# One plan of step places over the attention and gate stage of a packed-attention, SwiGLU and bilinear kernel

## The chip, the cores and the metric

The kernel runs on one core of one Trainium2 chip. The metric is device time in microseconds (us) of one execution, as the median over several runs. All work, the conversion of the weights included, is inside that time.

## The reference

The inputs are q, k and v of 8 batches, 8 heads, 576 positions and 64 values a head, and 32 packing queries p per head; then weights for two dense layers.

```python
p_packed = softmax(p @ k.T / 8) @ v            # 32 rows a head
x  = softmax(q @ p_packed.T / 8) @ p_packed    # 576 rows a head
x  = x laid out as 4608 tokens x 512
xn = x / sqrt(mean(x * x) + 1e-6) * rms_g
y  = (silu(xn @ w_gate) * (xn @ w_val)) @ w_out      # 512 -> 1536 -> 512
out = ((y @ w1) * (y @ w2)) @ w3 @ w_out2            # 512 -> 1024 -> 512
```

The weights arrive as 64-bit words and are turned to float32 on the chip. A dense product is done as three float32r products of high and low parts (hi x hi, hi x lo, lo x hi).

## The kernel before, in words

Only the first third of the kernel, the front and the dense gate stage of the 8 batches, is touched. What comes behind it (the product with `w_out`, the products of the weights, the last two layers) stays as it is.

**The work of a batch** has three parts, and each is a Python generator whose `yield`s cut it into steps:

- `pack(b)`, 7 steps. Steps 0 and 1: scores of p against k on TensorE (L216, all 32 matmuls in step 0), their maximum on VectorE and exponential on ScalarE, for one half of the heads each. Step 2: the load of k of batch b+2, transposes (L232) and their evictions (L236, L239). Step 3: the product with v (L247) and the load of v of batch b+1. Step 4: eviction (L256). Step 5: a transpose (L259), the block-diagonal `bdP1T` (L264) and `gP1T` (L266). Step 6: the Gram matrix `G` (L276, L279).
- `unpack(b)`, 18 steps. Step 0: scores of q (L305) and two 32 x 32 transposes on VectorE (L309). Step 1: the load of q of batch b+2, a maximum on VectorE; steps 2 to 4: subtraction, exponential and the other half. Steps 5 and 6: sums and reciprocals on VectorE (L321 to L323), a product on GpSimd (L324). Steps 7 and 8: transposes on VectorE (L329), one of them also shifted over partitions by two DMAs into `turned` (L332, L333). Step 9: the product with `G` on TensorE (L345); steps 9 and 10: its elementwise products `sq` on VectorE (L350). Step 11: from batch 3 on the two halves of `sq` are added on GpSimd (L354). Step 12: the sums of squares as matmuls against a column of ones (L361): 5 on the added halves, or 10 on both halves where nothing was added; `ssq` on VectorE (L363). Step 13: the power -0.5 on GpSimd (L366). Steps 14 and 15: transposes of it on TensorE (L371), the scaling on VectorE (L373). Steps 16 and 17: the split into `ah` and `al` (L59, L60).
- `dense_units`, 48 steps a batch, 6 blocks of 8. A step is 6 matmuls of 128x288 into one of 4 PSUM banks (L435). An even step ends with a tanh on ScalarE (L441) and a product on VectorE (L442), an odd one with `ht`: on VectorE in batch 0 (L447), on ScalarE and GpSimd in the others (L450, L451). Every fourth step an `ht` tile (3 buffers) is full, and its store goes out 8 steps later. After the fourth step of a block, `wb_unit` makes the weight products of the next block (L393 on TensorE, `wbh` on ScalarE, `wbl` on VectorE; both by the helper `split`, L59 and L60).

**Beside these** run two streams of weight conversion. A c step brings a load and two ScalarE operations (L115, L116), a d step the two VectorE operations (L122, L123) and the GpSimd addition (L125) for the gate and value weights; a d step that finds no converted words makes the c step itself. An o step is a whole conversion of a tile of `w_out`, w1 or w2: a load of 512 KB three tiles ahead, the same five operations, and a later store.

**The order** of all instructions is the order in which the Python code makes them, for each engine and for the DMA queue of SyncE (SP), which issues every load and store in order. Ahead of the dense stage a string names the generators one after the other ("p", "u": pack and unpack of batch 0; "P", "U": of batch 1; "c", "d": conversion; "l": loads of k, v, q of batches 1 to 3 in that order; "w": the first `wb_unit`; "x": four matmuls of the identity into a bank that nobody reads). Then `planned` runs the dense steps and after step n takes every step that has n in its list, in the order of the lists:

```python
    def planned(main, *others):
        for n, _ in enumerate(main):
            for at, gen in others:
                for _ in range(at.count(n)):
                    next(gen, None)
        for _, gen in others:
            drain(gen)
```

In the kernel before there is one such plan for batches 0 and 1 (steps 0 to 95), one call of `planned` for each of batches 2 to 6 (steps 0 to 47), and one for batch 7 with the first loads of the stage behind. While batch b is in the dense stage, `unpack(b+1)` and `pack(b+2)` are taken.

Of the kernel before, what the change touches and what calls it, by code (L numbers as in the profile page):

```python
# [16 lines left out]
B, H, S, D = 8, 8, 576, 64  # L17
NP = 32
R = 5
# [13 lines left out]
def packed_attention_swiglu_bilinear(ctx: ExitStack, tc, qT, kT, v, v_end, pT, rms_g, w_gv, w_out,  # L33
# [21 lines left out]
    def bank():  # L55
        return ps.tile([128, 512], F32, tag="gv", name="gv", bufs=4)
# [39 lines left out]
    def load_v(b):  # L96
        if b < B:
# [1 line left out]
            nc.sync.dma_start(out=vt[:, :R - 1], in_=v[b])  # L99
            nc.sync.dma_start(out=vt[64:, R - 1], in_=v_end[b])  # L100
            raw["v", b] = vt

    def load64(src):
# [23 lines left out]
    def converting(jobs, take):  # L130


        n64 = ahead64[0]
        ahead = [load64(src) for src, *_ in jobs[:n64]]
        yield
        for i, job in enumerate(jobs):
            take(ahead.pop(0), *job[1:])
            if i + n64 < len(jobs):
                ahead.append(load64(jobs[i + n64][0]))
            yield  # L140
# [145 lines left out]
    def unpack(b):  # L286
# [13 lines left out]
        for a, t in enumerate(ts):  # L300
            for c in range(NC):
                for e in range(2):
# [4 lines left out]
                                     start=True, stop=True, tile_position=(64 * e, r))  # L307
# [31 lines left out]
        for a in range(2):  # L339
            for e in range(2):  # L340
                for c in range(NC):
                    r = place(c, e)
                    k = r if b == 0 else 32 * c
                    x = turned[k:k + 32] if b and e else a2T[k:k + 32, e]
                    nc.tensor.matmul(ts[e][r:r + 32, a, :HALF], lhsT=G[k:k + 32, b % 2, e],  # L345
                                     rhs=x[:, HALF * a:HALF * a + HALF],
                                     start=True, stop=True, tile_position=(k, r))
        over.add(("G", b))
        for e in range(2):
            nc.vector.tensor_tensor(out=halves(sq[:, e]), in0=ts[e][:, :, :HALF], in1=halves(a2T[:, e]),  # L350
                                    op=ALU.mult)
            yield
        if b > 2:
            nc.gpsimd.tensor_tensor(out=sq[:, 0], in0=sq[:, 0], in1=sq[:, 1], op=ALU.add)  # L354
        yield
        ssq = att.tile([128, R], F32, tag="ssq", name="ssq")
        rinv = att.tile([128, R], F32, tag="rinv", name="rinv")
        t = slot("at")
        for r in range(R):
            for e in range(1 if b > 2 else 2):  # L360
                nc.tensor.matmul(t[:, 0, 2 * r:2 * r + 2], lhsT=sq[:, e, T0[r]:T0[r] + 128], rhs=ones,  # L361
                                 start=(e == 0), stop=(e == 1 or b > 2), skip_group_check=True)
        nc.vector.tensor_scalar(out=ssq, in0=t[:, 0, :2 * R].rearrange("p (r j) -> p r j", j=2)[:, :, 0],  # L363
                                scalar1=0.0, scalar2=1e-6, op0=ALU.max, op1=ALU.add)
        yield
# [19 lines left out]
    def wb_unit(b, g):  # L385
        gP1T = res["gP1T", b]
        while not all((g, c) in converted for c in range(NC)):
            next(gvd)
        t = slot("at")
        for c in range(NC):  # L390
            for e in range(2):
                r = place(c, e)
                nc.tensor.matmul(t[r:r + 32, e, :], lhsT=gP1T[64 * e:64 * e + 64, c, :],  # L393
                                 rhs=wgv[64 * e:64 * e + 64, c, :, 256 * g:256 * g + 256],
                                 start=True, stop=True, tile_position=(64 * e, r), skip_group_check=True)
        hi = dp.tile([128, 2, 512], F32R, tag="wbh", name="wbh", bufs=2)
        lo = dp.tile([128, 2, 512], F32R, tag="wbl", name="wbl", bufs=2)
        split(hi, lo, t, nc.vector)
        wb[b, g] = (hi, lo)
# [4 lines left out]
    def store_later(steps, **dma):  # L404
        held.append([steps, dma])

    def stores():
        for x in held:
            x[0] -= 1
        while held and held[0][0] <= 0:  # L410
            nc.sync.dma_start(**held.pop(0)[1])
# [2 lines left out]
        while held:  # L414
            stores()

    FIRST = [(b, g) for b in range(2) for g in range(6)]
    blocks = FIRST + [(b, g) for b in range(2, B) for g in range(6)]
    follow = dict(zip(blocks, blocks[1:]))

    def dense_units(blocks):
        for b, g in blocks:
            ah, al = res["a2n", b]
            hi, lo = wb.pop((b, g))
            for f in range(2):
                ht = dp.tile([128, 2, HALF], F32, tag="ht", name="ht", bufs=3)
                for hf in range(2):
                    th = dp.tile([128, HALF], F32, tag="th", name="th", bufs=3)
                    vl = dp.tile([128, HALF], F32, tag="vl", name="vl", bufs=2)
                    for i in range(2):  # L430
                        t = bank()
                        n = 0
                        for w, x in ((hi, ah), (hi, al), (lo, ah)):
                            for e in range(2):
                                nc.tensor.matmul(t[:, :HALF],  # L435
                                                 lhsT=w[:, e, 256 * i + 128 * f:256 * i + 128 * f + 128],
                                                 rhs=x[:, e, HALF * hf:HALF * hf + HALF],
                                                 start=(n == 0), stop=(n == 5))
                                n += 1
                        if i == 0:  # L440
                            nc.scalar.activation(out=th, in_=t[:, :HALF], func=AF.Tanh, scale=0.5)  # L441
                            nc.vector.scalar_tensor_tensor(out=th, in0=th, scalar=1.0, in1=t[:, :HALF],  # L442
                                                           op0=ALU.add, op1=ALU.mult)
                            stores()
                            yield 0.75
                    if b == 0:
                        nc.vector.scalar_tensor_tensor(out=ht[:, hf], in0=th, scalar=0.5, in1=t[:, :HALF],  # L447
                                                       op0=ALU.mult, op1=ALU.mult)
                    else:
                        nc.scalar.activation(out=vl, in_=t[:, :HALF], func=AF.Copy, scale=0.5)  # L450
                        nc.gpsimd.tensor_tensor(out=ht[:, hf], in0=th, in1=vl, op=ALU.mult)  # L451
                    if hf == 1:
                        store_later(4, out=hT_d[2 * g + f, :, S * b:S * b + S],
                                    in_=ht.rearrange("p a n -> p (a n)"))
                    yield 0.75
                    if (f, hf) == (0, 1) and (b, g) in follow:
                        wb_unit(*follow[b, g])

    def batch(b):
        return dense_units([(b, g) for g in range(6)])  # L460

    def some(gen, n):
        for _ in range(n):
            yield next(gen, None)

    def drain(gen):
        for _ in gen:
            pass
# [33 lines left out]
    def wb_first():  # L502
        wb_unit(0, 0)
        yield

    def later():
        for b in (1, 2, 3):
            load_k(b)
            yield
            if b < 3:  # L510
                load_v(b)
                yield
            load_q(b)
            yield

    jobs = [(w_out[128 * i:128 * i + 128, :], wo_d[128 * i:128 * i + 128, :]) for i in range(NF)]
    for n in range(16):
        r, c = GROUPS[n // 4]
        w, kk = ((w1, r), (w1, r + 2), (w2, r), (w2, r + 2))[n % 4]
        jobs.append((w[128 * kk:128 * kk + 128, 512 * c:512 * c + 512], w12_d[n]))  # L520
    ow = converting(jobs, out_weight)
    def spin():
        while True:
            t = bank()
            for _ in range(4):
                nc.tensor.matmul(t[:, :128], lhsT=ident, rhs=ident, start=True, stop=True)
            yield

    gens = dict(x=spin(), p=pack(0), u=unpack(0), c=gvw, d=gvd, w=wb_first(), l=later(), P=pack(1), U=unpack(1),
                Q=pack(2), V=unpack(2), R=pack(3), o=ow)  # L530
    for x in ("xppxdxpcpxdcpdpcxcdcuducpduxuxuxcxd"
              "xculdxuxxxxwxucudxxuuuxuPPxuuuuxudPl"):
        next(gens[x], None)
    for x in "pu":
        drain(gens[x])
    PLAN = [("P", [6, 9, 12, 21]),
# [8 lines left out]
    planned(dense_units(FIRST),  # L545
            *((at, gens[x] if x != "o" else some(ow, len(at))) for x, at in PLAN))
    for x in "PUQVRcdl":
        drain(gens[x])

    PACK = [7, 7, 16, 31, 32, 40, 43]  # L550
    UNPACK = [0, 1, 3, 4, 6, 11, 13, 15, 17, 24, 24, 25, 31, 32, 40, 41, 42, 44]
    for b in range(2, B - 1):
        others = [(UNPACK, unpack(b + 1)), ([9, 18, 23, 28, 35, 46], some(ow, 6))]
        if b + 2 < B:
            others.insert(0, (PACK, pack(b + 2)))
        planned(batch(b), *others)
    drain(ow)
    flush()
    att_ctx.close()
# [100 lines left out]
    def halved(w, hi, lo):  # L660
# [1 line left out]
            split(*behind.pop(), nc.vector)  # L662
            staged.append(0)
        behind.append((hi, lo, as_f32(w)))

    ORDER = (0, 5, 4, 6, 1, 3, 2)
# [149 lines left out]
    flush()  # L818
    p2_ctx.close()
    cv2_ctx.close()  # L820

    wt = ctx.enter_context(tc.tile_pool(name="wt", bufs=1, side="right"))
# [293 lines left out]
```

## Time and profile before

| | |
|---|---|
| median of 3 runs | 1357.19 us (1355.32 to 1358.64) |
| the profiled execution | 1356.66 us, its span 1354.4 us, granted clock 0.994 |
| TensorE matmul busy | 1327.6 us, 98% of the span |
| TensorE weight load busy | 1130.0 us, 83% |
| VectorE busy | 837.4 us, 62% |
| ScalarE, GpSimd busy | 580.1 us, 581.2 us |
| share of the chain that ended last | TensorE 89%, VectorE 4%, ScalarE 2%, GpSimd 2%, DMA 2% |

The profile is of one execution. Times are from the start of its span. Busy times of TensorE are modelled for their ends, so idle time and the granted clock (1 is 2.4 GHz, 0.5 is 1.2 GHz) tell more than its busy share. A wait is put down to what was released last. The dense stage of batch 0 starts at 49.72 us, that of batch 7 near 450 us (the first load of its plan, L572, is issued at 450.44).

### The profile page before, as it was taken

The page shows a single profiled execution, that of the slowest core. Times are in us where ns is not written, and L with a number is a line of the kernel's source. Part 1 is how long each engine was busy: PE and PEld are TensorE (multiplying, and loading weights), DVE is VectorE, ACT ScalarE, POOL GpSimd, SP SyncE. Part 2 cuts the span into 40 slices and gives each one's busy share as a digit, 9 for nine tenths or more (in the row PEclk, how much of TensorE's full clock was granted, in tenths as well). Part 3 has the DMA queues.
Part 4 walks back from the last instruction along what each step waited for, and adds up shares of the span by engine and source line. Part 5 has one row for each costly group of instructions (what it writes and reads, how often), then busy time and mean ns, then how long its engine had stood idle before and what let it go on. Part 6 is the DMA issues. An engine that isn't in the chain of part 4 may idle for free.

```text
span 1354.4 us, 23647 instructions
## 1 busy us (share of the span) xinstructions
PE 1327.6 (98%) x9022; PEld 1130.0 (83%) x9022; DVE 837.4 (62%) x1261; ACT 580.1 (43%) x1117; POOL 581.2 (43%) x490
## 2 busy tenths in 40 slices
PE   7979999999999999999999999999999999999998
PEld 6768878788788888888888888888888888899998
DVE  6785676676766557726375564566468357457444
ACT  5544566666766656525243342125015103305113
POOL 3341446556556543203131213447345535535543
PEclk9989999999999999999999999999999999999999
DMA  8664637666352467734299875656755855787875
GB/s 309 252 223 171 238 135 263 230 217 216 116 190 104 149 220 245 236 106 140 86 372 389 337 261 210 228 206 226 279 198 199 283 191 210 242 310 258 280 270 186
DMA packets 88705, 304.03 MB, mean 224 GB/s; under 512 B 9872, under 2 KB 14992, under 8 KB 74384
## 3 DMA queue, kind: packets, MB, share of 16 engines
q1 hardware_dynamic: 88592, 302.52, 63.3%
q8 instruction: 71, 1.16, 0.3%
q14 instruction: 42, 0.34, 0.1%
HBM read 223.87 MB, written 76.55 MB: 222 GB/s over the span
## 4 chain that ended last, share of the span: by engine, by line
PE 89%; DVE 4%; ACT 2%; POOL 2%; DMA 2%; issue 1%; SPq 0%; ACTq 0%; DVEq 0%; POOLq 0%
PE gv L435 20%; PE at L641 14%; PE gv L954 13%; PE at L954 13%; PE gv L641 7%; PE gv L1048 6%; PE at L1048 5%; PE gv L742 3%; PE at L393 3%; POOL sl L60 1%; DMA hT_d<-ht 1%; PE at L361 1%; PE at L345 1%; PE at L247 1%; DVE wbl L60 1%
## 5 line engine op out<-in xcount | busy, mean ns | idle before, releaser
L451 POOL TENSOR_TENSOR ht<-th,vl 128x288 f32<-128x288 f32 x168 | 141.8, 851 | 142.7 <-ACT vl L450 60.3
L435 PE MATMUL gv<-ah,wbh 128*128 128x288 f32 x768 | 175.3, 309 | 3.8 <-DVE ht L447 1.8
L435 PEld LDWEIGHTS gv<-ah,wbh 128*128 128x128 f32 x768 | 121.4, 189 | 55.1 <-issue 22.6
L435 PE MATMUL gv<-ah,wbl 128*128 128x288 f32 x768 | 165.0, 296 | 2.2 <-DVE wbl L60 2.2
L435 PE MATMUL gv<-al,wbh 128*128 128x288 f32 x768 | 165.4, 296 | 0.3 <-DVE al L60 0.3
L60 DVE TENSOR_TENSOR hl<-hr,hh 128x512 fp32r<-128x512 f32 x108 | 100.7, 938 | 74.7 <-ACT hh L59 74.4
L980 POOL TENSOR_TENSOR s<-uc 128x512 f32<-128x512 f32 (+1 forms) x40 | 49.0, 1224 | 217.8 <-DVE uc L936 217.8
L954 PE MATMUL gv<-xh,w 128*128 128x512 f32 (+1 forms) x560 | 137.8, 367 | 0.0
L954 PE MATMUL at<-xh,w 128*128 128x512 f32 (+1 forms) x560 | 137.7, 367 | 0.0
L125 POOL TENSOR_TENSOR c_o<-c_o,c_y 128x512 int32<-128x512 int32 x52 | 71.4, 1372 | 146.2 <-DVE c_o L123 115.2
L435 PEld LDWEIGHTS gv<-ah,wbl 128*128 128x128 f32 x768 | 123.7, 189 | 3.1 <-DVE wbl L60 3.1
L435 PEld LDWEIGHTS gv<-al,wbh 128*128 128x128 f32 x768 | 124.0, 189 | 0.5 <-DVE al L60 0.5
L442 DVE SCALAR_TENSOR_TENSOR th<-th,gv 128x288 f32<-128x288 f32 x192 | 85.4, 446 | 58.0 <-ACT th L441 46.4
L59 ACT ACTIVATE hh<-hr 128x512 fp32r<-128x512 f32 x108 | 67.8, 631 | 114.3 <-PE at L641 56.7
L954 PEld LDWEIGHTS gv<-xh,w 128*128 128x128 f32 x560 | 102.5, 188 | 13.4
L954 PEld LDWEIGHTS at<-xh,w 128*128 128x128 f32 x560 | 102.5, 188 | 13.2
L641 PE MATMUL at<-hl,wo_h 128*128 128x512 f32 x288 | 112.1, 389 | 0.0
L641 PE MATMUL at<-hh,wo_l 128*128 128x512 f32 x288 | 112.1, 389 | 0.0
L641 PE MATMUL at<-hh,wo_h 128*128 128x512 f32 x288 | 112.1, 389 | 0.0
L441 ACT ACTIVATE th<-gv 128x288 f32<-128x288 f32 x192 | 78.9, 411 | 54.4 <-PE gv L435 53.9
L450 ACT ACTIVATE vl<-gv 128x288 f32<-128x288 f32 x168 | 69.2, 412 | 63.4 <-PE gv L435 45.6
L60 POOL TENSOR_TENSOR xl<-yi,xh 128x1024 fp32r<-128x1024 f32 (+1 forms) x20 | 55.2, 2758 | 71.6 <-ACT xh L59 47.8
(163 smaller groups left out, 2828.7 us busy)
## 6 DMA issues: line engine op xcount, KB each, us to landing
w<-ws_d SPq DMA_DIRECT2D x40, 1024.0 KB, 4.9
w<-w_d SPq DMA_DIRECT2D x35, 1024.0 KB, 4.8
w<-ws_d SPq DMA_DIRECT2D x40, 768.0 KB, 4.5
hT_d<-ht SPq DMA_DIRECT2D x96, 288.0 KB, 4.0
hr<-hT_d SPq DMA_DIRECT2D x108, 256.0 KB, 4.6
w<-in_w_gv_dram SPq DMA_DIRECT2D x24, 512.0 KB, 6.7
w<-in_w_out_dram SPq DMA_DIRECT2D x20, 512.0 KB, 7.0
q<-in_qT_dram SPq DMA_DIRECT2D x8, 1152.0 KB, 6.6
```

The source lines that it names most:

```text
L59: nc.scalar.activation(out=hi, in_=src, func=AF.Copy)
L60: eng_lo.tensor_tensor(out=lo, in0=src, in1=hi.bitcast(F32), op=ALU.subtract)
L125: nc.gpsimd.tensor_tensor(out=d, in0=d, in1=shape(y), op=ALU.add)
L435: nc.tensor.matmul(t[:, :HALF], lhsT=w[:, e, 256 * i + 128 * f:256 * i + 128 * f + 128], rhs=x[:, e, HALF * hf:HALF * hf + HALF], start=(n ...
L441: nc.scalar.activation(out=th, in_=t[:, :HALF], func=AF.Tanh, scale=0.5)
L442: nc.vector.scalar_tensor_tensor(out=th, in0=th, scalar=1.0, in1=t[:, :HALF], op0=ALU.add, op1=ALU.mult)
L450: nc.scalar.activation(out=vl, in_=t[:, :HALF], func=AF.Copy, scale=0.5)
L451: nc.gpsimd.tensor_tensor(out=ht[:, hf], in0=th, in1=vl, op=ALU.mult)
L641: nc.tensor.matmul(acc[m], lhsT=w[:, kk, 128 * m:128 * m + 128], rhs=x, start=(kk == 0 and a == 0), stop=(kk == NF - 1 and a == 2))
L954: nc.tensor.matmul(t, lhsT=wi[:, r, pos, a], rhs=x[:, j, r, :w], start=(start and at == 0), stop=(at == 5), skip_group_check=True)
L980: nc.gpsimd.tensor_tensor(out=s2, in0=u2, in1=c22, op=ALU.mult)
L1048: nc.tensor.matmul(t, lhsT=wi[:, s, k, 128 * m:128 * m + 128], rhs=x, start=(j in (0, 5, 4, 3) and k == 0 and n == 0), stop=(k == 3 and n ...
```

## The change

The string of the front is put in another order. One plan now covers the dense steps of batches 0 to 6 (steps 0 to 335); batches 2 to 6 use the same lists with 48 b added, and two steps of `unpack` now lie one step ahead of their batch (-1). All lists hold as many places as their generators have steps, and the draining between batches is gone. The halves of the squares are added on GpSimd from batch 1 on.

```diff
-        if b > 2:
+        if b:
             nc.gpsimd.tensor_tensor(out=sq[:, 0], in0=sq[:, 0], in1=sq[:, 1], op=ALU.add)
...
-            for e in range(1 if b > 2 else 2):
+            for e in range(1 if b else 2):
...
-    for x in ("xppxdxpcpxdcpdpcxcdcuducpduxuxuxcxd"
-              "xculdxuxxxxwxucudxxuuuxuPPxuuuuxudPl"):
+    for x in ("xpxpdxxcppxdpcdpcducducdpcuuxxcxudculx"
+              "dxxuxxxwxuudxcxxxuuuxuuPxPuuuxudPlcdlP"):
...
-    PLAN = [("P", [6, 9, 12, 21]),
-            ("U", [13, 14, 15, 16, 17, 18, 19, 20, 22, 23, 24, 28, 32, 40, 40, 41, 41, 42]),
-            ("c", [0, 0, 5, 6, 13, 16, 18, 21, 23, 26, 26, 28, 32, 33, 36]),
-            ("d", [0, 3, 4, 7, 11, 12, 15, 17, 20, 22, 22, 23, 24, 30]),
-            ("l", [0, 7, 13, 16, 66, 81, 84]),
-            ("Q", [46, 46, 50, 56, 56, 62, 70]),
-            ("V", [65, 65, 67, 68, 72, 73, 74, 77, 81, 82, 82, 82, 85, 85, 87, 87, 89, 90]),
-            ("R", [77, 77, 81, 84, 87, 91, 92]),
-            ("o", [50, 83])]
+    PLAN = [("P", [3, 9, 21]),
+            ("U", [14, 15, 15, 16, 17, 18, 19, 20, 22, 24, 24, 28, 32, 32, 40, 42, 42, 46]),
+            ("c", [0, 5, 6, 13, 16, 16, 23, 23, 26, 27, 27, 32, 33, 36]),
+            ("d", [3, 4, 7, 11, 12, 15, 17, 20, 22, 22, 23, 24, 28]),
+            ("l", [9, 15, 16, 69, 69, 86]),
+            ("Q", [46, 46, 49, 51, 53, 58, 63]),
+            ("V", [65, 65, 67, 70, 72, 73, 74, 77, 79, 82, 82, 82, 85, 85, 87, 88, 89, 90]),
+            ("R", [77, 77, 81, 85, 88, 92, 95]),
+            ("o", [39, 86])]
...
-    PACK = [7, 7, 16, 31, 32, 40, 43]
-    UNPACK = [0, 1, 3, 4, 6, 11, 13, 15, 17, 24, 24, 25, 31, 32, 40, 41, 42, 44]
+    UNPACK = [-1, -1, 0, 0, 7, 11, 13, 16, 17, 24, 24, 26, 32, 33, 36, 40, 42, 44]
+    PACK = [6, 6, 15, 30, 34, 38, 45]
+    WOUT = [16, 20, 24, 25, 34, 38]
+    steps = [(at, gens[x]) for x, at in PLAN]
     for b in range(2, B - 1):
-        others = [(UNPACK, unpack(b + 1)), ([9, 18, 23, 28, 35, 46], some(ow, 6))]
         if b + 2 < B:
-            others.insert(0, (PACK, pack(b + 2)))
-        planned(batch(b), *others)
+            steps.append(([48 * b + n for n in PACK], pack(b + 2)))
+        steps.append(([48 * b + n for n in UNPACK], unpack(b + 1)))
+        steps.append(([48 * b + n for n in WOUT], ow))
+    planned(dense_units(blocks[:6 * (B - 1)]), *steps)
```

## Rows read from the trace of the kernel before

**Rows 1.** The page, part 1: busy time, share, instructions of each engine.

```profile
PE 1327.6 (98%) x9022; PEld 1130.0 (83%) x9022; DVE 837.4 (62%) x1261; ACT 580.1 (43%) x1117; POOL 581.2 (43%) x490
```

**Rows 2.** Waits of TensorE, 49.7 to 460 us: total, times, longest.

```profile
PE at L345 <- DVE a2T L329: 4.9, 1, 4.9
PE gv L435 <- DVE wbl L60: 2.2, 4, 0.8
...
```

**Rows 3.** Busy time by stretch; columns PE, PEld, DVE, ACT, POOL, clock, DMA, GB/s.

```profile
75.00:84.00 9.00, 3.50 (x35) 2.66 (x34) 7.99 (x17) 4.83 (x10) 3.62 (x3) 1.00 0.60 244
84.00:92.00 8.00, 5.88 (x47) 4.47 (x48) 7.79 (x13) 4.05 (x7) 4.06 (x3) 0.57 0.81 269
...
98.40:106.00 7.60, 7.60 (x58) 6.24 (x57) 3.03 (x8) 0.98 (x3) 2.44 (x2) 0.78 0.14 53
46.00:53.00 7.00, 6.53 (x47) 5.84 (x47) 5.68 (x12) 5.70 (x12) 1.20 (x1) 0.93 0.01 4
53.00:80.00 27.00, 23.68 (x297) 18.22 (x295) 23.87 (x48) 17.61 (x35) 10.52 (x10) 1.00 0.97 358
```

**Rows 4.** TensorE in order of time, batch 0: start, us, operation, [idle before].

```profile
49.72 0.53 PE L435 MATMUL gv<-ah,wbh 128*128 128x288 f32 x2
...
57.20 1.32 PE L247 MATMUL at<-vt,a1T 128*32 128x64 f32 x80
...
76.31 0.53 PE L435 MATMUL gv<-ah,wbh 128*128 128x288 f32 x2 [1.20 <-DVE ht L447]
...
86.12 1.13 PE L345 MATMUL at<-a2T,G 32*32 32x288 f32 x5 [4.93 <-DVE a2T L329]
...
91.65 0.42 PE L435 MATMUL gv<-ah,wbh 128*128 128x288 f32 x2
...
92.44 0.43 PE L435 MATMUL gv<-ah,wbh 128*128 128x288 f32 x2
```

**Rows 5.** VectorE in order of time, batch 0.

```profile
68.65 0.45 DVE L447 SCALAR_TENSOR_TENSOR ht<-th,gv 128x288 f32<-128x288 f32 x1 [0.92 <-DMA hT_d<-ht]
...
75.80 0.45 DVE L447 SCALAR_TENSOR_TENSOR ht<-th,gv 128x288 f32<-128x288 f32 x1 [1.14 <-DMA hT_d<-ht]
...
85.21 0.77 DVE L329 STREAM_TRANSPOSE a2T<-a 128x576 f32<-128x576 f32 x1
...
87.58 1.63 DVE L123 SCALAR_TENSOR_TENSOR wgv<-c_h,c_t 128x512 int32<-128x512 int32 x1
```

**Rows 6.** ScalarE in order of time, ahead of the dense stage.

```profile
50.28 0.70 ACT L239 ACTIVATE a1T<-at 128x640 f32<-128x640 f32 x1
```

**Rows 7.** SP's queue in order of time, the load of q of batch 1.

```profile
35.71 17.53 SPq L108 DMA_DIRECT2D w<-in_w_gv_dram  x2
53.29 0.43 SPq L87 DMA_DIRECT2D q<-in_qT_dram  x1
```

**Rows 8.** The sums of squares on TensorE: batch 1, batch 4.

```profile
98.42 2.29 PE L361 MATMUL at<-ones,sq 128*128 128x2 f32 x20
...
271.77 1.28 PE L361 MATMUL at<-ones,sq 128*128 128x2 f32 x10
```

**Rows 9.** TensorE's two idle times in the dense stage of batch 3.

```profile
252.10 0.53 PE L435 MATMUL gv<-ah,wbl 128*128 128x288 f32 x2 [0.78 <-DVE wbl L60]
...
267.86 0.53 PE L435 MATMUL gv<-ah,wbh 128*128 128x288 f32 x2 [0.84 <-ACT vl L450]
```

**Rows 10.** VectorE ahead of the first of them.

```profile
247.59 0.88 DVE L122 TENSOR_SCALAR c_t<-c_h 128x512 int32<-128x512 int32 x1 [0.35 <-ACT c_h L115]
248.51 0.69 DVE L123 SCALAR_TENSOR_TENSOR c_o<-c_h,c_t 128x512 int32<-128x512 int32 x1
...
250.88 1.16 DVE L60 TENSOR_TENSOR wbl<-at,wbh 128x1024 fp32r<-128x1024 f32 x1
```

**Rows 11.** GpSimd in order of time: a conversion, an addition of squares.

```profile
87.16 1.51 POOL L125 TENSOR_TENSOR wgv<-wgv,c_y 128x512 int32<-128x512 int32 x1 [1.18 <-DVE wgv L123]
...
213.01 1.45 POOL L354 TENSOR_TENSOR sq<-sq 128x576 f32<-128x576 f32 x1
```

More of the change, by code (lines that the diff above doesn't have):

```diff
@@ L359, in unpack @@
         for r in range(R):
-            for e in range(1 if b > 2 else 2):
+            for e in range(1 if b else 2):
                 nc.tensor.matmul(t[:, 0, 2 * r:2 * r + 2], lhsT=sq[:, e, T0[r]:T0[r] + 128], rhs=ones,
-                                 start=(e == 0), stop=(e == 1 or b > 2), skip_group_check=True)
+                                 start=(e == 0), stop=(e == 1 or b > 0), skip_group_check=True)
         nc.vector.tensor_scalar(out=ssq, in0=t[:, 0, :2 * R].rearrange("p (r j) -> p r j", j=2)[:, :, 0],
@@ L415, in flush @@
             stores()
-    FIRST = [(b, g) for b in range(2) for g in range(6)]
-    blocks = FIRST + [(b, g) for b in range(2, B) for g in range(6)]
+    blocks = [(b, g) for b in range(B) for g in range(6)]
     follow = dict(zip(blocks, blocks[1:]))
@@ L535, in packed_attention_swiglu_bilinear @@
         drain(gens[x])
-    PLAN = [("P", [6, 9, 12, 21]),
[8 rows of a table removed]
[L545 to L548, printed above, removed]
-    PACK = [7, 7, 16, 31, 32, 40, 43]
-    UNPACK = [0, 1, 3, 4, 6, 11, 13, 15, 17, 24, 24, 25, 31, 32, 40, 41, 42, 44]
+    PLAN = [("P", [3, 9, 21]),
[8 rows of a table added]
+    UNPACK = [-1, -1, 0, 0, 7, 11, 13, 16, 17, 24, 24, 26, 32, 33, 36, 40, 42, 44]
+    PACK = [6, 6, 15, 30, 34, 38, 45]
+    WOUT = [16, 20, 24, 25, 34, 38]
+    steps = [(at, gens[x]) for x, at in PLAN]
     for b in range(2, B - 1):
-        others = [(UNPACK, unpack(b + 1)), ([9, 18, 23, 28, 35, 46], some(ow, 6))]
         if b + 2 < B:
-            others.insert(0, (PACK, pack(b + 2)))
-        planned(batch(b), *others)
+            steps.append(([48 * b + n for n in PACK], pack(b + 2)))
+        steps.append(([48 * b + n for n in UNPACK], unpack(b + 1)))
+        steps.append(([48 * b + n for n in WOUT], ow))
+    planned(dense_units(blocks[:6 * (B - 1)]), *steps)
     drain(ow)
```

## The prediction

> **What bounds the kernel now.** I read the busy shares first: TensorE is busy for 98% of the span [rows 1], so only two things can shorten the kernel: less TensorE work, or less of the idle and slow time that is left. The change touches nothing behind batch 6, so I looked at TensorE's waits in the dense stage before that. The largest is one wait of 4.9 us of the products with `G` for a transpose on VectorE; four waits for `wbl` make 2.2 us [rows 2]. Then I placed them with the busy times by stretch. From 75 to 84 us TensorE does 3.50 us of work in 9, with VectorE at 7.99; from 84 to 92 it does 5.88 us in 8, with VectorE at 7.79 and a mean clock of 0.57 [rows 3]. So in batch 0 VectorE is the bound, for it carries the gate weights' conversion, `ht` and unpack of batch 1 at once, and TensorE, which can be at most four banks ahead, waits for it. Later batches run at full clock with about one wait each.
>
> In those two stretches TensorE stands still for 5.5 + 2.1 = 7.6 us, and loses about 2.5 us to the clock: 0.43 x 2 of 8 us is 6.9 us at 1.2 GHz, and it works in about 5 of them, from 86.12 on. From 98.4 to 106 the clock is 0.78, which is 3.3 us at 1.2 GHz with TensorE busy throughout, so 1.7 us more are lost [rows 3]. This fall comes after the sums of squares of batch 1, 2.29 us of matmuls with two columns each [rows 8].
>
> **Squares added on GpSimd.** Batches 1 and 2 now have 5 matmuls in place of 10, as batches 3 to 7 have: 2.29 us becomes 1.28 us [rows 8], 1.0 us each, 2.0 us in all, on TensorE, which is the bound there. The two additions take 1.45 us each on GpSimd [rows 11]. A dense step is 92.44 - 91.65 = 0.79 us of TensorE [rows 4]; batch 1 gives the addition the steps 24 to 32, batch 2 the steps 82 to 85. That is 6.3 and 2.4 us, so I cost it at nothing. Without that cover the 5 matmuls would wait at most for one conversion of 1.51 us and the addition, 3 us a batch.
>
> **The way to the dense stage.** VectorE takes the steps of pack 0, conversions and unpack 0 in the same sequence as before; only ScalarE's conversions, the spinning matmuls (22 in place of 21) and unpack's step 13 change places. I take 0, and between -0.8 and +0.8 us: about one group of spinning matmuls more or less in front of a transpose. At its end pack 1's step 3, the load of q of batch 1, a c and a d step now come before dense step 0. Step 3 needs both evictions; the second ends at 50.28 + 0.70 = 50.98 [rows 6]. Then its matmuls, 1.26 us to the next start [rows 4], put dense step 0 at 52.2 in place of 49.72, 2.5 us later. Half of that is work that was done at step 6 before. VectorE meanwhile does the d step's 1.1 us, but must then wait for the first dense steps. Written out step by step, its queue is 1.2 us later than before by step 8.
>
> **The queue of loads.** Before, q of batch 1 (1152 KB) is issued at 53.29, behind two loads of gate weights that blocked SP for 17.53 us [rows 7]; the second waits for a c step which lay in the dense stage. The DMA engines idle at a share of 0.01 from 46 to 53 us and are full, 0.97 at 358 GB/s, from 53 to 80 [rows 3]. After, q comes behind only the first of the two, near 36 us: it leaves the full stretch 1152 KB / 358 GB/s = 3.3 us emptier. In that stretch VectorE waited for stores of `ht`, 0.92 us at dense step 13 and 1.14 us at step 17 [rows 5]. Also, v of batch 2 moves from step 13 to 15, behind the store that goes out at step 14. I take both waits as gone. The first 0.92 and the step `gP1T`, now ahead of step 12, repay the 1.2 us; from step 17 on VectorE is 1.1 us earlier.
>
> **The bubble.** The transpose that ends it finished at 85.21 + 0.77 = 85.98 [rows 5]; it finishes near 84.8. Unpack's step 9 is at dense step 24 in place of 23, so one dense step fits into the wait. From there VectorE still has the same list to go through, so TensorE gains what VectorE gained, plus the 0.4 us that it had in hand: 1.5 us in all by step 33. Nothing is queued behind the addition on GpSimd but one conversion. If the store waits stay, VectorE is 1.2 us late instead, and the loop start isn't paid back.
>
> **The clock.** With the bubble shorter but not gone I leave the first low stretch as it is. The second follows 2.29 us of thin matmuls that become 1.28; I take half of the 1.7 us, 0.85, between 0 and 1.7.
>
> **Batches 1 to 6.** TensorE's idle times there: 2.2 us before `wbl` [rows 2], one of 0.84 us behind `ht` [rows 9], and one of 0.4; 3.4 us. The first kind sits at dense step 17. In front of its `wbl` at 250.88 VectorE does a conversion of 0.88 + 0.69 us [rows 10], and the unpack steps of dense steps 0 to 11. The o step at 9 goes away to 16 and two unpack steps move into the batch before; the wait of 0.78 us [rows 9] is shorter than the conversion, so it goes. The 0.84 us comes from a store of `ht` behind `turned` on SP's queue, which waits for transposes that are late for the same crowd; they come earlier, so do the stores. What is late next is the new cluster: at 24 and 25 two o steps and two products `sq` are 4.6 us of VectorE. TensorE has the matmuls with `G`, 1.2 us, and a `wb_unit`, 1.1 us, in that time and four banks; counted out, the product of step 26 ends some 6.2 us after step 24 begins, and step 30, which needs its bank, would start at 7.1. So it fits by 0.9 us. Loads: w at 16, 20, 24, 25, k at 15 (before 16), v at 30 (31), q at -1 (1) are the same bytes, closer together, and SP has the stores of `ht` between them. I take 2.5 of the 3.4 us as gone, between -1 and 3.4.
>
> **Sum.** 2.0 + 1.5 + 0.85 + 2.5 = 6.85 us off the profiled execution's 1356.66 (its span 1354.4 and 2.3 around it): 1349.8. The median lies 0.5 above that execution, so I forecast 1350.3 us.
>
> **Rivals.**
> 1. *The front doesn't pay back.* The stores of `ht` still land late (k of batch 2 stands before the first of them, as it did), VectorE stays 1.2 us behind, the clock falls twice, and half of the `wbl` waits come back elsewhere: 2.0 - 1.2 + 0 + 1.2 = 2.0 us gained, 1355.2. For it: 0.97 DMA share to 80 us [rows 3]. Against: the idle stretch that q moves into.
> 2. *The cluster at steps 24 and 25 becomes the wait, on the slower side.* A VectorE operation of a conversion took 1.63 us at 87.58, where 0.69 is usual, beside a GpSimd conversion that ran from 87.16 to 88.67 [rows 5, 10, 11]: 0.94 us more. If all four conversion operations of the cluster meet GpSimd, that is 3.8 us, 0.9 of which fit; 2.9 us in each of batches 2 to 6 is 14.4 us: 1364.7. It decides from the first blocked operation on; each further one costs 4.7 us, and three of the four still leave 1360. Against: GpSimd has its own conversions behind VectorE's, so only some can meet.
>    The Trainium skill (SBUF — State Buffer, section Terms) says that VectorE and GpSimd arbitrate for a port pair, that the lock is "held for the full instruction", and that the loser blocks; the row at 87.58 agrees, ending 0.5 us after the GpSimd operation. By that rule the two new additions alone could cost VectorE 1.45 us each, which would make the forecast up to 2.9 us later.
> 3. *The bubble goes altogether.* VectorE's queue gets ahead far enough that the first low stretch of the clock goes too: 2.5 us, the other 0.85 of the second, and 1.5 of the idle time: 1345.5. Against: VectorE is busy 7.8 to 8 us in 8 or 9 [rows 3] and does the same list.
>
> **How the numbers follow.** Forecast 0.55, rival 1 0.24, rival 2 0.06, rival 3 0.15. The bound of "no change" is 0.3%, 4.07 us: faster is below 1353.1. The forecast's own spread (prologue 0.8, clock 0.85, waits 1 to 2) is 1347 to 1353.5, nearly all faster; with rival 3 and a little of the others that makes 0.70. Rival 1 and the forecast's upper edge are "same", 0.25; rival 2 is slower, 0.05. The range 1344.5 to 1356 takes in rivals 1 and 3 and leaves rival 2 out.
>
> **What would show it.** Right: L361 with 10 records in batches 1 and 2; q of batch 1 issued before 46 us; no wait of VectorE for a store of `ht` at steps 13 and 17; the wait before L345 in batch 0 at 2 to 3 us; no low clock after the thin matmuls; no waits for `wbl` at step 17. Wrong: dense step 0 later than 53 us with a bubble as long as before; new waits of TensorE behind L442 near step 30 of batches 2 to 6; GpSimd's additions late for L361. If batch 7 starts less than 4 us earlier than now, the forecast fails.

## The result and the profile after

The changed kernel takes 1368.28 us (median of 4, 1364.12 to 1371.58) beside 1357.30 us for the kernel before (median of 4); the ratio is 1.0088 [1.0071, 1.0106], with the 95% interval in brackets here and below. It is 11 us slower where 7 us less were forecast. By the prediction's own sign, batch 7 should start at least 4 us earlier; it starts 6.5 us later.

The profiled execution is the fastest of the four: 1364.12 us, its span 1362.3, against 1356.66 and 1354.4. Lines have moved: L435 is now L432, L442 is L439, L123 is L121, L354 is L352, L361 is L359. The page's first part hardly differs from [rows 1]; it is too coarse for what happened:

```profile
PE 1330.1 (98%) x9010; PEld 1131.4 (83%) x9010; DVE 835.6 (61%) x1261; ACT 578.1 (42%) x1117; POOL 583.6 (43%) x492
```

What tells is where each batch's dense stage begins, read off the time line (the first matmul of its step 0, in us; a column for each batch, and the last from the start of batch 2 to that of batch 7):

| kernel | 0 | 2 | 3 | 4 | 5 | 6 | 7 | 2 to 7 |
|---|---|---|---|---|---|---|---|---|
| before | 49.7 | 178.0 | 232.8 | 288.9 | 343.4 | 397.9 | 448.3 | 270.3 |
| changed | 52.3 | 175.6 | 231.9 | 290.4 | 347.9 | 406.2 | 454.8 | 279.1 |

Up to batch 2 the change gains 2.4 us. Batches 2 to 5, the four that have six o steps each, then lose 1.5, 2.4, 3.0 and 3.7 us; batch 6, where the conversions run out, gains 1.8. Another 1.4 us is lost behind the start of batch 7.

One thing has to be reckoned into this table. The first step of each unpack has moved over the border into the batch before, with 1.2 us of TensorE. Batches 2 to 5 each give one away and get one; but batch 1 now has two, and batch 6 none. Unpack 3, in the kernel before and in the changed one:

```profile
178.88 1.20 PE L305 MATMUL at<-q,bdP1T 64*32 64x288 f32 x32
174.34 1.34 PE L303 MATMUL at<-q,bdP1T 64*32 64x288 f32 x32
```

So for the same work the change gains 3.6 us up to batch 2, batch 6 gains 0.6, and batches 2 to 6 lose 10.0 us, not 8.8. Every kernel with the new places of unpack is to be compared with the one before in this way: 1.2 us are to be added to its column "2 to 7".

The waits of TensorE in the dense stage, as in [rows 2] (engine, line, what was waited for, total, times, longest):

```profile
PE gv L432 <- DVE th L439: 4.5, 6, 1.7
PE at L359 <- POOL sq L352: 3.0, 4, 0.8
PE at L343 <- DVE a2T L327: 2.5, 1, 2.5
PE gv L432 <- ACT vl L447: 1.9, 2, 1.0
PE gv L432 <- DVE wbl L60: 1.4, 4, 0.3
```

The bubble of batch 0 is halved in name, 2.5 us in place of 4.9, and the waits for `wbl` are smaller. New are four waits for the halves of the squares, one in each of batches 2 to 5. What VectorE itself waits for, from 106 to 460 us, has two lines that the kernel before doesn't have, the last two here:

```profile
DVE th L439 <- ACT th L438: 42.1, 53, 3.0
DVE wbl L60 <- ACT wbh L59: 28.9, 28, 3.3
DVE th L439 <- POOL ht L448: 14.8, 8, 2.2
DVE c_o L121 <- DMA w_d<-c_o: 9.8, 4, 3.5
DVE c_o L121 <- DMA wo_d<-c_o: 9.3, 4, 2.9
```

Eight times, twice in each of the four batches, the second VectorE operation of a weight conversion stands until a store of an earlier `c_o` has landed, 19.1 us together. `c_o` has two buffers. The o step at 24 needs that of step 16 back, the one at 25 that of step 20. Batch 4, VectorE in order of time:

```profile
317.88 1.42 DVE L348 TENSOR_TENSOR sq<-at,a2T 128x576 f32<-128x576 f32 x2 [0.17 <-PE at L343]
319.22 0.56 DVE L120 TENSOR_SCALAR c_t<-c_h 128x512 int32<-128x512 int32 x1
322.71 0.69 DVE L121 SCALAR_TENSOR_TENSOR c_o<-c_h,c_t 128x512 int32<-128x512 int32 x1 [2.93 <-DMA w_d<-c_o]
323.51 0.43 DVE L120 TENSOR_SCALAR c_t<-c_h 128x512 int32<-128x512 int32 x1
326.56 0.69 DVE L121 SCALAR_TENSOR_TENSOR c_o<-c_h,c_t 128x512 int32<-128x512 int32 x1 [2.62 <-DMA w_d<-c_o]
327.17 0.44 DVE L439 SCALAR_TENSOR_TENSOR th<-th,gv 128x288 f32<-128x288 f32 x1
327.53 1.22 DVE L60 TENSOR_TENSOR wbl<-at,wbh 128x1024 fp32r<-128x1024 f32 x1
```

Everything behind them waits in order: the product of dense step 26 (L439), which frees a PSUM bank, runs at 327.17, and `wbl` of the next block after it. On GpSimd the addition of the squares (L352) stands behind the conversions' own additions. TensorE, same batch:

```profile
326.32 0.53 PE L432 MATMUL gv<-ah,wbh 128*128 128x288 f32 x2 [1.04 <-ACT vl L447]
327.67 0.54 PE L432 MATMUL gv<-ah,wbh 128*128 128x288 f32 x2 [0.28 <-DVE th L439]
328.80 0.53 PE L432 MATMUL gv<-ah,wbl 128*128 128x288 f32 x2 [0.34 <-DVE wbl L60]
330.08 1.28 PE L359 MATMUL at<-ones,sq 128*128 128x2 f32 x10 [0.75 <-POOL sq L352]
```

The clock makes it worse. These short waits and the thin matmuls after them are followed, in two of the four batches of this execution (3 and 5), by a stretch at 1.2 GHz; there they cost twice. Batches 2 and 4, the latter with the waits shown, have no such fall, and no run shows what decides between them. After the sums of squares of batch 1 the fall of [rows 3] is gone, as hoped (stretches; the clock is the third column from the end):

```profile
98.40:106.00 7.60, 7.60 (x67) 6.60 (x67) 4.84 (x11) 2.22 (x5) 2.45 (x2) 1.00 0.63 186
271.90:275.20 3.30, 3.30 (x15) 3.30 (x15) 0.53 (x2) 0.98 (x3) 1.70 (x3) 0.50 0.95 302
388.00:391.20 3.20, 3.20 (x14) 3.20 (x14) 0.53 (x2) 0.63 (x2) 1.87 (x4) 0.50 0.64 175
```

The mean clock of the four executions was 0.993, 0.987, 0.988 and 0.986. The profiled one is that with 0.993; by these means the others have about 16 us more at 1.2 GHz (an estimate: 0.006 x 1366 us x 2), of which half is lost; they are 3.5 to 7.5 us slower.

### The profile page after: what moved, and what is told of

It reads as the page before. It is cut to its first block, busy times and chain, and to the rows that moved or that the text cites. A ratio compares the mean times of both kernels' runs of the same rounds, so it can differ in the third digit from the quotient of the medians.

```text
span 1362.3 us, 23638 instructions
## 1 busy us (share of the span) xinstructions
PE 1330.1 (98%) x9010; PEld 1131.4 (83%) x9010; DVE 835.6 (61%) x1261; ACT 578.1 (42%) x1117; POOL 583.6 (43%) x492
## 4 chain that ended last, share of the span: by engine, by line
PE 73%; DMA 3%; POOL 2%; DVE 2%; issue 1%; ACT 0%; SPq 0%; DVEq 0%; POOLq 0%; ACTq 0%
PE at L946 13%; PE gv L946 13%; PE at L636 12%; PE gv L432 12%; PE gv L636 7%; PE gv L1040 5%; PE at L1040 5%; PE gv L736 3%; PE at L391 2%; POOL sl L60 1%; DMA w_d<-c_o 1%; DMA hr<-hT_d 1%; DMA wo_d<-c_o 1%; DVE hl L60 1%; POOL xl L60 0%
## 5 line engine op out<-in xcount | busy, mean ns | idle before, releaser
L432 PE MATMUL gv<-ah,wbh 128*128 128x288 f32 x768 | 177.8, 313 | 7.2 <-DVE th L439 4.5
L432 PEld LDWEIGHTS gv<-ah,wbh 128*128 128x128 f32 x768 | 122.0, 190 | 59.6 <-DVE th L439 19.7
L432 PE MATMUL gv<-ah,wbl 128*128 128x288 f32 x768 | 165.4, 296 | 1.4 <-DVE wbl L60 1.4
L432 PE MATMUL gv<-al,wbh 128*128 128x288 f32 x768 | 165.7, 297 | 0.0
L123 POOL TENSOR_TENSOR c_o<-c_o,c_y 128x512 int32<-128x512 int32 x52 | 71.5, 1375 | 166.9 <-DVE c_o L121 140.5
L439 DVE SCALAR_TENSOR_TENSOR th<-th,gv 128x288 f32<-128x288 f32 x192 | 85.4, 447 | 67.2 <-ACT th L438 49.0
L432 PEld LDWEIGHTS gv<-ah,wbl 128*128 128x128 f32 x768 | 124.2, 190 | 2.3 <-DVE wbl L60 2.3
L432 PEld LDWEIGHTS gv<-al,wbh 128*128 128x128 f32 x768 | 124.6, 190 | 0.0
```

The costliest lines, as they stand in the source:

```text
L123: nc.gpsimd.tensor_tensor(out=d, in0=d, in1=shape(y), op=ALU.add)
L432: nc.tensor.matmul(t[:, :HALF], lhsT=w[:, e, 256 * i + 128 * f:256 * i + 128 * f + 128], rhs=x[:, e, HALF * hf:HALF * hf + HALF], start=(n ...
```

## The experiments

The theory is that the stores of `c_o` lose the time, for their buffers come free too late. There are two rivals: A, the VectorE load of the cluster of steps 24 and 25 with GpSimd in its way (the prediction's rival 2); and B, the front or the additions. Each ratio is to runs of the kernel before that were taken beside that experiment: medians of 1355.47 us for e1 to e4, 1356.16 for e5 to e8, and 1356.74 for e9 and e10.

**e1_spread.** `-WOUT = [16, 20, 24, 25, 34, 38]`, `+WOUT = [9, 18, 23, 28, 35, 46]` in the changed kernel.

> The changed kernel with the six places of the o steps (conversions of w_out, w1, w2) put back to those of the kernel before, 9, 18, 23, 28, 35 and 46; all else as changed. Theory (store): the product c_o of a conversion has two buffers, its store is held for 8 steps, and the o steps at 24 and 25 want the buffers of 16 and 20 back after 8 and 5 steps; VectorE stands in order behind that store. Then the 8 waits of VectorE for the stores of c_o (19.1 us in the changed kernel) are gone, batches 2 to 5 are back near 55 us each from 56.3 to 58.5, and the time is 1351 to 1356 us. Rival A (load): the cluster of VectorE work at 24 and 25 and its blocking by GpSimd is too much by itself; the same time, so this run does not part the two. Rival B (front or additions): the front or the earlier additions on GpSimd lose the time; then it stays over 1362 us.

1353.68 us, ratio to before 0.9988 [0.9979, 0.9997]. No wait for `c_o` is left, and batches 2 to 6 take 268.3 us. B falls; A is not parted from the theory by this run.

**e2_three_buffers.** `-c_o_bufs = [2]`, `+c_o_bufs = [3]`; nothing is moved.

> The changed kernel with three buffers in place of two for c_o, all places as changed. Theory (store): step 24 then wants a buffer that was stored in the batch before, and step 25 that of 16, 9 steps back; the waits for stores of c_o fall from 19.1 us to under 6 us and the time to 1352 to 1359 us. Rival A (load): the same operations stand at the same places, so it stays at 1363 to 1369 us. Rival B (front or additions): stays over 1362 us.

1352.15 us, 0.9973 [0.9962, 0.9984]: 16 us off the changed kernel by one buffer. One wait of 1.5 us for `c_o` is left in place of eight; batches 2 to 6 take 265.5 us, and TensorE has no idle time in them. The stretch of batch 4, in the kernel before, in the changed kernel and with three buffers (columns as in [rows 3]):

```profile
288.90:343.40 54.50, 54.16 (x604) 45.24 (x603) 38.50 (x71) 36.55 (x82) 32.73 (x35) 1.00 0.60 207
```

```profile
290.40:347.90 57.50, 55.08 (x610) 45.38 (x602) 39.03 (x71) 36.00 (x81) 32.75 (x35) 1.00 0.58 197
```

```profile
287.00:341.20 54.20, 54.20 (x611) 45.27 (x603) 40.68 (x71) 35.97 (x81) 33.37 (x35) 1.00 0.60 209
```

The same work stands at the same places, so A falls too, though what it says does happen: the conversions of the cluster take 1.18 and 1.67 us in place of 0.69, and the slack holds them.

```profile
316.52 1.18 DVE L121 SCALAR_TENSOR_TENSOR c_o<-c_h,c_t 128x512 int32<-128x512 int32 x1
317.80 0.43 DVE L120 TENSOR_SCALAR c_t<-c_h 128x512 int32<-128x512 int32 x1
318.26 1.67 DVE L121 SCALAR_TENSOR_TENSOR c_o<-c_h,c_t 128x512 int32<-128x512 int32 x1
319.86 0.44 DVE L439 SCALAR_TENSOR_TENSOR th<-th,gv 128x288 f32<-128x288 f32 x1
```

**e3_cluster_in_before.** In the kernel before, `-[9, 18, 23, 28, 35, 46]`, `+[16, 20, 24, 25, 34, 38]`.

> The kernel before with only the six places of the o steps changed to 16, 20, 24, 25, 34 and 38. Theory (store): the same waits of VectorE for stores of c_o come up, 15 to 20 us in four batches, and the time rises by 6 to 12 us to 1363 to 1369 us. Rival A (load): rises as well, but without idle time of VectorE in front of the conversions. Rival B (front or additions): within 2 us of the kernel before.

1375.03 us, 1.0149 [1.0133, 1.0165]: the six numbers alone cost 20 us, more than I expected. The waits come up, more of them than said (15.2 + 10.6 = 25.8 us where 15 to 20 were), and the clock falls once in each of batches 2 to 5 (and once in batch 1); two of the stretches:

```profile
DVE c_o L123 <- DMA wo_d<-c_o: 15.2, 5, 3.6
DVE c_o L123 <- DMA w_d<-c_o: 10.6, 5, 4.3
```

```profile
282.30:285.50 3.20, 3.20 (x15) 3.20 (x14) 0.45 (x1) 1.62 (x6) 1.75 (x2) 0.50 0.96 331
336.90:340.10 3.20, 3.20 (x85) 2.75 (x84) 0.96 (x3) 0.41 (x1) 2.42 (x4) 0.50 0.02 5
```

**e4_additions_in_before.** In the kernel before, `-if b > 2:`, `+if b:`, and the matmuls to match.

> The kernel before with only the halves of the squares added on GpSimd from batch 1 on. By the prediction's term: 5 matmuls fewer in batches 1 and 2, 1.0 us each, and perhaps one fall of the clock less (1.7 us): 1353.5 to 1355.5 us. Rival: the sums wait for GpSimd as long as they are shorter, so nothing: 1357 us. Rival B: the additions block VectorE or come late by more than they save: over 1359 us.

1353.07 us, 0.9986 [0.9978, 0.9995], so 1.9 us [0.7, 3.0] less, and the second fall of the clock is gone from this execution:

```profile
98.40:106.00 7.60, 7.60 (x66) 6.60 (x67) 4.85 (x11) 2.16 (x4) 2.44 (x2) 1.00 0.20 79
```

No trace with the additions from batch 1 on, of the eight here, has that fall. Of the four without, three have it and one (e7) doesn't; so the additions are not the only thing that decides on it, and how much of the 1.9 us is clock stays open.

**e5_front_only.** The string and `PLAN` of the changed kernel in the kernel before.

> The kernel before with only the string of the front and the plan of batches 0 and 1 from the changed kernel; additions from batch 3 on and places of batches 2 to 6 as before. By the prediction's term: 1.5 us gained in the bubble, 0 on the way to it, so 1355 us beside 1355.5 to 1357 of before. Rival (not paid back): dense step 0 starts 2.5 us later, VectorE still waits for a store of ht (0.59 us in the changed kernel) and the bubble ends where it did; then the start of batch 2 doesn't come before 177 us and the time is 1356 to 1359 us.

1357.15 us, 1.0011 [0.9999, 1.0023]; batch 2 starts at 180.1, where it started at 178.0 before. The new front gains nothing. That it loses 1.5 us is likely, but the interval takes in no change.

**e6_old_front_new_lists.** The old string and `PLAN` in the changed kernel, `c_o_bufs = [3]`.

> The changed kernel with the string of the front and the plan of batches 0 and 1 of the kernel before, and three buffers for c_o; the additions from batch 1 on and all places of batches 2 to 6 as changed. If the new front gains nothing, this is the fastest: 174 us to batch 2 as in the run with the additions alone, 54.25 us for each of the batches 2 to 5 as with three buffers: 1347 to 1351 us. Rival: the new front is worth its 1.5 us, and this is slower than the changed kernel with three buffers (1352.15), at 1353 to 1355 us.

1350.68 us, 0.9960 [0.9948, 0.9972]: 5.4 us faster than the kernel before. It has the lowest time of all versions, though the interval overlaps that of e2.

**e7_lists_only.** The places of `UNPACK` and `PACK` alone: old front, additions from batch 3 on, o steps as before.

> The kernel before with only the places of unpack and pack in batches 2 to 6 from the changed kernel (in one plan); front, additions and o steps (9, 18, 23, 28, 35, 46) as before. By the prediction's term the waits for wbl at dense step 17 and behind ht go, 2.5 us: 1353 to 1355 us. Rival: with the o step still at 9 the waits for wbl stay, and nothing is gained: 1355.5 to 1357.5 us.

1355.64 us, 0.9992 [0.9983, 1.0002]: at the edge of nothing. The waits for `wbl` at step 17 are gone, and batches 2 to 6 take 268.4 in place of 270.3 us, of which 1.2 is the step moved into batch 1. The 0.7 us left is less than the runs can tell from no change.

**e8_store_at_once.** `-store_later(4, out=dst, ...)`, `+store_later(1, out=dst, ...)` for `c_o` in the changed kernel.

> The changed kernel with the stores of c_o held for 2 dense steps in place of 8; two buffers, all places as changed. Theory (store held too long): the stores of the o steps at 16 and 20 leave at 18 and 22, before the products of 24 and 25 want their buffers; the waits of VectorE for them fall from 19.1 to 4 to 10 us and the time to 1353 to 1360 us. Rival (landing alone is late): the stores land some 6 us after their issue in any case, SP is blocked for longer by waiting for GpSimd, and the time stays over 1362 us.

1368.09 us, 1.0087 [1.0072, 1.0101], with 19.8 us of waits, about as many as without the edit. My edit missed its aim: the list of held stores goes out in order, so the store stayed behind those of `ht` and SP's order didn't change. But the trace answers part of the question. In batch 4, SP (start, time, issue):

```profile
318.94 0.90 SPq L409 DMA_DIRECT2D w_d<-c_o  x1
319.93 3.43 SPq L106 DMA_DIRECT2D w<-in_w_dram  x2
323.45 0.38 SPq L409 DMA_DIRECT2D hT_d<-ht  x1
323.93 0.40 SPq L409 DMA_DIRECT2D w_d<-c_o  x1
```

VectorE gets the two buffers at 327.41 and 331.27, 8.4 and 7.3 us after the issues; the data had been ready 0.9 and 1.5 us before those. The hold isn't what is late. In front of the first store SP had stood for the transposes that `turned` copies, and then issued two loads of weights and two stores of `ht` within 2 us.

**e9_store_direct.** `-store_later(4, out=dst, in_=as_f32(w))`, `+nc.sync.dma_start(out=dst, in_=as_f32(w))`.

> The changed kernel with the stores of c_o issued by SP right behind their conversion, past the list in which they waited behind the stores of ht (the run with a hold of 2 steps had left them behind that list, so their order on SP was the same); two buffers, all places as changed. Theory 1 (order on SP): the store of step 20 now stands before the loads of 24 and 25; if its place on SP is what is late, VectorE's waits fall from 19.1 to under 10 us and the time to 1353 to 1361 us. Theory 2 (landing): data are ready at 318.0 and 322.5 us in the run before this, are issued 0.9 and 1.5 us later, and land 8.4 and 7.3 us after that; then the order gives 1 to 2 us a batch at most, VectorE's waits stay at 12 to 19 us, and the time at 1361 to 1368 us.

1371.72 us, 1.0105 [1.0086, 1.0124]. Half of each theory: all eight waits of VectorE are gone and the stores land after 2.2 us in the median (4.3 in the changed kernel), as theory 1 has it, yet no time is gained. SP now stands for each conversion, the stores of `ht` behind are late, and GpSimd waits for them, with the power of the sums (L364) queued behind:

```profile
POOL ht L448 <- DMA hT_d<-ht: 38.3, 13, 5.4
```

```profile
PE at L369 <- POOL rinv L364: 14.4, 4, 3.8
```

**e10_one_place.** `-WOUT = [16, 20, 24, 25, 34, 38]`, `+WOUT = [16, 20, 24, 30, 34, 38]`.

> The changed kernel with the o step at 25 put to 30, two buffers. Both theories of the store: only the step at 24 still asks for its buffer too early (8 steps after 16), so about half of the 8 waits stay, 9 to 12 us of VectorE, and the time lies between, 1356 to 1363 us. Rival A (load): with the cluster taken apart nothing is lost, 1352 to 1355 us.

1357.76 us, 1.0005 [0.9996, 1.0014]: between, as both theories of the store had it, though seven waits (18.4 us) are left and not four. The four of step 24 are there as expected, 10.8 us. The other three, 7.6 us, are new: step 34 waits for the buffer of step 24, ten steps back; the changed kernel has no wait there. Against e2, the seven waits cost 4 to 6 us, where the eight of the changed kernel cost 16. The clock is a good part of that: in batches 2 to 6 TensorE stands idle for 7.0 us here and 7.3 in the changed kernel, but here its clock doesn't fall in them.

## Why the prediction was wrong

1. **The failed step** is the one in "Batches 1 to 6" that costs the new cluster at nothing: "it fits by 0.9 us". It added up VectorE's own operations and TensorE's banks, and called the loads "the same bytes, closer together". It never asked when the two buffers of `c_o` come free. The kernel before uses a buffer again after 10 to 22 steps, the changed one after 8 and 5. That they would collide was in the code and needed no trace: two buffers, a hold of 8 steps, and o steps at 16, 20, 24, 25. How long the wait is was not: the landing decides it, up to 8.4 us. In place of the 0.9 us to spare stand 19.1 us of VectorE's waits; e2 shows that they and their sequel on the clock are worth 16 us, and e3 that the six numbers are enough to bring them about.
2. **Rival 2** named the place and the rows that would show it (waits behind L442 near step 30), but a wrong mechanism: with e2 the blocked conversions fit. That its 1364.7 us lie near the measured time is luck; it also counts five batches, and batch 6 has no o step at 25. By the Trainium skill (SBUF — State Buffer, section Terms), the lock on the port pair that VectorE and GpSimd share lasts for the whole instruction; the 1.67 us of e2 agree, for that operation ends at 319.93, 0.5 us after a GpSimd conversion. That this makes the two new additions cost time doesn't show: e4 is faster.
3. **The additions** were right within the noise: 2.0 us of matmuls and 0.85 of the clock forecast, 1.9 [0.7, 3.0] measured, and the fall after the thin matmuls of batch 1 is gone from every trace that has them.
4. **The front** came out as rival 1: where 1.5 us were to be gained, e5 is 1.5 us [-0.1, 3.1] slower. Dense step 0 starts at 52.28 (forecast 52.2), and q of batch 1 is issued at 36.7. The first agreement is luck: the split into `ah` and `al` ends 0.6 us later than before, and the evictions with it, but the product with v starts at 50.99 behind the first eviction and not, as reckoned, behind both:

```profile
50.99 1.36 PE L245 MATMUL at<-vt,a1T 128*32 128x64 f32 x80 [0.48 <-ACT a1T L234]
```

   Then 0.59 us of waiting for a store of `ht` at step 13 is left, and the transpose that ends the bubble finishes at 85.16 + 0.77 = 85.93, where 84.8 was forecast and 85.98 was before:

```profile
69.38 0.45 DVE L444 SCALAR_TENSOR_TENSOR ht<-th,gv 128x288 f32<-128x288 f32 x1 [0.59 <-DMA hT_d<-ht]
84.42 0.45 DVE L444 SCALAR_TENSOR_TENSOR ht<-th,gv 128x288 f32<-128x288 f32 x1 [0.25 <-DMA hT_d<-ht]
85.16 0.77 DVE L327 STREAM_TRANSPOSE a2T<-a 128x576 f32<-128x576 f32 x1
```

   The wait in front of L343 is half as long only because TensorE came to it later. What stands in the tail of the front was not tested by itself.
5. **The lists** were right in kind and somewhat too small in size: 2.5 us forecast. With the third buffer batches 2 to 6 take 4.8 us less than before, of which 1.2 is the step moved into batch 1, so 3.6 us; and TensorE has no idle time there, where it had 3.2 us. The additions' 1.9 and these 3.6 make 5.5 us, and e6, which has these two and not the new front, is 5.4 us faster.
6. The loss behind the start of batch 7, 1.4 us in the profile, stays open. From there to the end the twelve traces take 906.0 to 907.6 us, and no run tests it.

## What to carry to other kernels

Where a plan moves a step, write down for each of its buffers when the one before it comes free: number of buffers times spacing, against the hold of the store, its place on the queue and its landing. The engine's own load was the smaller half of the question here, for VectorE works in order, and its wait for one buffer became the wait of everything behind it. And a bound by TensorE with little idle time is fragile: in two of four batches short waits and thin matmuls were followed by a fall of its clock, and cost more than they lasted.

## What the runs showed of the hardware

The time from issue to landing of the same store of 256 KB was 2.2 us in the median when it was issued right behind its conversion (e9), and up to 8.4 us when two loads and two stores had been issued on the same queue within the 2 us before it (e8). And TensorE's clock fell to 1.2 GHz once in each of batches 1 to 5 of e3, though the engine's longest wait there was 3.0 us; in the changed kernel two falls followed waits of at most 0.84 us each. In e10 as much idle time was followed by no fall.
